# Loading the second half of batch 0's k through GpSimd's queue with a cast, instead of through ScalarE's queue and a ScalarE cast

## The chip, the core and the metric

The kernel runs on one core of a Trainium2 chip. The core has TensorE (PE in the profile, with its weight loads as PEld), VectorE (DVE), ScalarE (ACT), GpSimd (POOL) and SyncE (SP), and 16 DMA engines that serve the queues of all of them. The metric is the time of one execution in device microseconds; lower is better. The shown runs of the kernel before have a median of 292.75 us (eleven runs, 292.6 to 294.3).

## The reference

An attention without softmax is followed by a layer-normalised two-layer network. All inputs and the output are float32.

```python
# q, k, v: (8 batches, 8 heads, 576 rows, 64)
kv  = einsum('bhsd,bhse->bhde', k, v)
out = einsum('bhsd,bhde->bhse', q, kv)
rms = sqrt(mean(out * out, axis=-1) + 1e-06)
attn = out / rms * g_norm
# x: attn with its heads joined, (8, 576, 512)
xn = (x - mean(x)) / sqrt(var(x) + 1e-06) * g_ln
out = x + maximum(xn @ w_ch1, 0.0) @ w_ch2        # 512 -> 2048 -> 512
```

For each head, `kv` needs every row of k and of v before q can be multiplied with it. So nothing of a batch but its transposes can start before its k and v are on the chip.

## The kernel before

TensorE works in bfloat16 and the inputs are float32, so each input is cast on its way. Nearly all of it is cast by the DMA itself: a load that GpSimd issues reads float32 from memory and writes bfloat16. Only batch 0's k is loaded otherwise. It goes as float32 into the tile `k_f`, by the hardware queues of SyncE (line 124, heads 0 to 3) and ScalarE (line 125, heads 4 to 7). VectorE casts the first half into `k_p` (line 467) and ScalarE the second (line 468). `k_p` and `v_p` are views of the bfloat16 tiles `k_in[0]` and `v_in[0]`. `pairs` (line 117) gives the access pattern of one half: 128 partitions with two runs of 2,304 bytes each, which are 256 packets and 576 KB of float32.

The order of every engine's instructions is the order of the program text (a manual schedule). At the start GpSimd issues, one after the other: the two halves of batch 0's v (lines 126 and 127), two parts of its q (line 129), the first quarter of the weights w1 (`load_w1(0)`, line 130), an identity matrix for transposes, the rest of q (line 132), and three more quarters of w1. Then come w2's first half, the loads of batch 1, and w2's second half (lines 157 to 161). A load waits for the landing of the load eight before it in the same kind of queue. SyncE issues, after `k_f`, two small rows: `gl_row` (line 141) and `gn_row` (line 145), the weights of the two norms. VectorE clears tiles meanwhile (lines 123 to 155). After its half of the cast it spreads the two rows over the partitions (lines 470 and 471).

TensorE begins with 18 matmuls on a cleared tile whose results nobody reads (`fill(18)`, line 475). Then `kv_first` (line 207) makes batch 0's kv in two halves: the first of heads 0 to 3, from the first halves of k and v, the second of heads 4 to 7. Each half is copied out by VectorE (lines 222, 224, 225) and ScalarE (line 223). Then q is transposed (`turn_groups`, line 177) and multiplied with kv (`half_o`, line 494), the sums of squares are made, and by 15.7 us the first matmul with w1 runs (line 402). From there to the end the two matmul loops of the network, `mm1` (line 392) and `mm2` (line 439), fill TensorE, and the attention of the later batches is planned into them by slots (`at`, `tick`).

The tile `k_f` takes a buffer of the pool `m1pool`, whose two buffers later hold the network's hidden layer.

Of the kernel before, what the change touches and what calls it, by code (L numbers as in the profile page):

```python
# [14 lines left out]
def kernel(  # L15
# [11 lines left out]
    nc = tc.nc  # L27
    f32 = mybir.dt.float32
# [5 lines left out]
    B, H, S, D = q.shape  # L34
# [5 lines left out]
    HP = H // 2  # L40
# [3 lines left out]
    J, JJ, JP = 4, 5, 9  # L44
# [9 lines left out]
    m1pool = ctx.enter_context(tc.tile_pool(name="m1pool", bufs=2))  # L54
# [23 lines left out]


    NP = HP * JP * D  # L80
    k_f = m1pool.tile([128, HP, JP * D], f32, tag="m1", name="k_f")
    k_p, v_p = (t.rearrange("p h j d -> p (h j d)")[:, :NP].rearrange(
        "p (hp n) -> p hp n", hp=HP) for t in (k_in[0], v_in[0]))
    gl_row = work.tile([128, Dm], f32, tag="sq", name="gl_row")
# [32 lines left out]
    def pairs(t, hp0, hp1):  # L117
        return bass.AP(tensor=t.tensor, offset=t.offset + hp0 * 2 * S * D,
                       ap=[[JP * D, 128], [2 * S * D, hp1 - hp0], [1, JP * D]])
# [1 line left out]
    fill_sb = consts.tile([128, 512], bf16)  # L121
    gate = consts.tile([1, 1], bf16)
    nc.vector.memset(fill_sb, 0.0)
    nc.sync.dma_start(k_f[:, :HP // 2], pairs(k, 0, HP // 2))
    nc.scalar.dma_start(k_f[:, HP // 2:], pairs(k, HP // 2, HP))
    nc.gpsimd.dma_start(v_p[:, :HP // 2], pairs(v, 0, HP // 2))
    nc.gpsimd.dma_start(v_p[:, HP // 2:], pairs(v, HP // 2, HP))
    for h0 in (0, H // 2):
# [335 lines left out]
        clock[0] += 1  # L464


    nc.vector.tensor_copy(k_p[:, :HP // 2], k_f[:, :HP // 2])
    nc.scalar.copy(k_p[:, HP // 2:], k_f[:, HP // 2:])
    del k_f
    nc.vector.stream_shuffle(g_norm_sb[:, 0, :], gn_row, [0] * 32)  # L470
    nc.vector.stream_shuffle(g_ln_sb, gl_row, [0] * 32)
# [212 lines left out]
```

## Time and profile before

| what | value |
|---|---|
| median of the shown runs | 292.75 us |
| time of the profiled execution | 292.96 us |
| its span, first to last instruction | 291.2 us |
| mean granted TensorE clock | 0.998 |
| TensorE matmul busy | 283.8 us, 97% of the span |
| ScalarE busy | 154.8 us, 53% |
| VectorE busy | 151.0 us, 52% |
| GpSimd busy | 41.2 us, 14% |
| moved by DMA | 35.84 MB, mean 123 GB/s |
| of it by GpSimd's queue | 17.76 MB |
| of it by SyncE's queue | 16.99 MB |
| of it by ScalarE's queue | 0.72 MB |

The span is 1.8 us shorter than the profiled execution's time; what lies outside it is the launch and the end of the program. In the profile, q0 is the queue of GpSimd (software), q1 that of SyncE and q10 that of ScalarE (hardware). The bytes of a DMA are counted on the side that it writes, so a casting load of 590 KB of float32 counts 288 KB. "Idle before" in an instruction's row is time that its engine stood still before it, with the work that ended last among what it waited for.

### The profile page before, as it was taken

Reading aid. Unit: us, or ns where it says so; the run is one execution under the profiler, and the core shown is the slowest. Engines: PE = TensorE matmul, PEld = TensorE weight load, DVE = VectorE, ACT = ScalarE, POOL = GpSimd, SP = SyncE. Lnnn points to the kernel's source line nnn. Section 1 sums busy time; section 2 is a strip of 40 time slices with the busy share of each in tenths; the row PEclk is TensorE's granted clock in tenths of the full one; section 3 lists DMA queues with packets and bytes.
Section 4 is the critical chain, followed back from the end, with each engine's and each line's share of the span. In section 5 each row is a group of like instructions: output and inputs, shape, how many; then the busy total and the mean of one; then the engine's idle time right before and its main releaser. Section 6 shows DMA issues by size and latency. Waiting matters only on the chain.

```text
span 291.2 us, 5801 instructions
## 1 busy us (share of the span) xinstructions
PE 283.8 (97%) x2320; PEld 159.1 (55%) x2320; DVE 151.0 (52%) x335; ACT 154.8 (53%) x341; POOL 41.2 (14%) x68
## 2 busy tenths in 40 slices
PE   8889999999999999999999999999999999999995
PEld 3579755995578644444444444444444444444444
DVE  5775028826996793765276936661678200220022
ACT  3467754985569832882188418920894066016500
POOL 8523520041050003100320023000000000000000
PEclk9999999999999999999999999999999999999999
DMA  7999999469799619993998279959202510131033
GB/s 216 203 206 202 200 202 221 98 110 192 144 146 202 98 37 158 211 166 70 155 202 127 56 146 201 147 78 164 54 18 56 108 36 0 38 80 28 0 74 72
DMA packets 63290, 35.84 MB, mean 123 GB/s; under 512 B 30748, under 2 KB 58268, under 8 KB 63264
## 3 DMA queue, kind: packets, MB, share of 16 engines
q0 software_dynamic: 28016, 17.76, 44.9%
q1 hardware_dynamic: 34736, 16.99, 29.3%
q10 hardware_dynamic: 512, 0.72, 0.7%
q8 instruction: 18, 0.29, 0.4%
q14 instruction: 8, 0.07, 0.1%
HBM read 36.71 MB, written 9.44 MB: 158 GB/s over the span
## 4 chain that ended last, share of the span: by engine, by line
PE 80%; DMA 7%; DVE 6%; ACT 2%; issue 2%; SPq 1%; POOL 0%; DVEq 0%; POOLq 0%
PE p L402 40%; PE p L418 33%; DMA qt<-q_p 4%; PE o_ps L260 2%; DMA v_in<-in_v_dram 2%; PE kv_ps L235 2%; DVE o_sb L423 1%; DVE ss L287 1%; DVE x_blk L311 1%; DVE y L292 1%; DMA out_dram<-o_sb 1%; ACT m L405 1%; PE tp L183 1%; DVE xc L321 1%; PE p L196 1%
## 5 line engine op out<-in xcount | busy, mean ns | idle before, releaser
L402 PE MATMUL p<-xT_blk,w_sb 128*128 128x128 bf16 (+2 forms) x1024 | 132.0, 286 | 0.5 <-ACT m L405 0.3
L418 PE MATMUL p<-w_sb,m 128*128 128x512 bf16 (+2 forms) x608 | 130.2, 368 | 0.0
L405 ACT ACTIVATE m<-p 128x512 bf16<-128x512 f32 x144 | 85.3, 597 | 45.2 <-PE p L402 43.4
L402 PEld LDWEIGHTS <-w_sb 128*128 128x128 bf16 x1024 | 78.6, 98 | 45.5 <-issue 1.1
L418 PEld LDWEIGHTS <-m 128*128 128x128 bf16 x608 | 56.5, 98 | 60.3
L423 DVE SCALAR_TENSOR_TENSOR o_sb<-p,rstd,x_blk 128x512 f32<-128x512 f32 (+2 forms) x38 | 27.3, 719 | 44.2 <-PE p L418 41.5
L266 ACT ACTIVATE sq<-o_ps 128x512 f32<-128x512 f32 x34 | 20.2, 594 | 39.0 <-PE o_ps L260 39.0
L287 DVE TENSOR_REDUCE ss<-sq 128x8 f32<-128x512 f32 x34 | 23.2, 682 | 19.9 <-ACT sq L266 19.9
L329 ACT ACTIVATE dev<-x_blk,st_blk 128x512 f32<-128x512 f32 x36 | 25.8, 718 | 6.2 <-DVE st_blk L315 6.1
L321 DVE SCALAR_TENSOR_TENSOR xc<-x_blk,st_blk,g_ln_sb 128x512 bf16<-128x512 f32 x34 | 25.6, 752 | 1.2
L292 DVE TENSOR_TENSOR y<-o_ps,inv 128x512 f32<-128x512 f32 x34 | 23.5, 692 | 2.6
L311 DVE SCALAR_TENSOR_TENSOR x_blk<-y,g_norm_sb 128x512 f32<-128x512 f32 x34 | 23.5, 692 | 1.2
L411 DVE RECIPROCAL rstd<-rstd 128x4 f32<-128x4 f32 x9 | 1.6, 175 | 39.3 <-ACT rstd L410 39.3
L304 DVE RECIPROCAL inv<-rms 128x8 f32<-128x8 f32 x36 | 7.2, 200 | 22.5 <-ACT rms L297 22.4
L98 POOL COPY gate<-qt 1x1 bf16<-1x1 bf16 x5 | 0.9, 178 | 115.1 <-DMA qt<-q_p 115.1
L297 ACT ACTIVATE rms<-ss,eps_sb 128x8 f32<-128x8 f32 x36 | 10.8, 300 | 7.8 <-DVE ss L287 7.1
L260 PEld LDWEIGHTS <-qt 128*128 128x128 bf16 (+1 forms) x152 | 9.7, 100 | 8.5 <-DMA qt<-q_p 2.1
L260 PE MATMUL o_ps<-kv_pack,qt 128*128 128x128 bf16 (+1 forms) x152 | 13.3, 221 | 0.6 <-DMA qt<-q_p 0.3
L196 PE MATMUL p<-fill_sb 128*128 128x512 bf16 x28 | 9.2, 491 | 1.2 <-DVE eps_sb L137 1.2
L339 ACT COPY xT_blk<-tp 128x512 bf16<-128x512 bf16 x10 | 5.8, 579 | 2.3 <-PE tp L337 2.3
L329 ACT ACTIVATION_READ_ACCUMULATOR dev<-x_blk,st_blk 128x1 f32 x36 | 6.9, 193 | 0.0
L238 ACT CAST kv_pack<-kv_ps 64x256 bf16<-64x256 f32 x7 | 2.6, 366 | 7.9 <-PE kv_ps L235 7.8
(79 smaller groups left out, 119.0 us busy)
## 6 DMA issues: line engine op xcount, KB each, us to landing
out_dram<-o_sb SPq DMA_DIRECT2D x70, 128.0 KB, 2.5
w_sb<-in_moe_w_ch_dram POOLq DMA_DIRECT2D x8, 512.0 KB, 14.1
k_in<-in_k_dram POOLq DMA_DIRECT2D x7, 320.0 KB, 5.2
v_in<-in_v_dram POOLq DMA_DIRECT2D x7, 320.0 KB, 9.0
q_in<-in_q_dram POOLq DMA_DIRECT2D x7, 320.0 KB, 13.2
q_in<-in_q_dram POOLq DMA_DIRECT2D x8, 256.0 KB, 12.6
k_in<-in_k_dram POOLq DMA_DIRECT2D x7, 256.0 KB, 6.7
v_in<-in_v_dram POOLq DMA_DIRECT2D x7, 256.0 KB, 11.9
```

The costliest lines, as they stand in the source:

```text
L196: nc.tensor.matmul(p1, lhsT=fill_sb[:, :128], rhs=fill_sb, start=True, stop=True)
L260: nc.tensor.matmul(flat[rows, hp * 128:(hp + 1) * 128], lhsT=lhsT_of(hp), rhs=kvp[:, hp, :], start=True, stop=True)
L266: nc.scalar.activation(self.sq_t, self.o_ps, func=AF.Square)
L287: nc.vector.tensor_reduce(self.ss, self.sq_t, axis=AX.X, op=ALU.add)
L292: nc.vector.tensor_mul(self.y_t, self.o_ps, self.inv().to_broadcast([128, H, D]))
L311: nc.vector.scalar_tensor_tensor(x_blk[:, ts].rearrange("p (h d) -> p h d", h=H), in0=self.y_t, scalar=1.0, in1=g_norm_sb.to_broadcast([12 ...
L321: nc.vector.scalar_tensor_tensor(self.xc_t, in0=x_blk[:, self.ts], scalar=st[:, 1, self.ts:self.ts + 1], in1=g_ln_sb, op0=ALU.add, op1=ALU ...
L329: nc.scalar.activation(dev, x_blk[:, ts], func=AF.Square, bias=st[:, 1, ts:ts + 1], accum_out=st[:, 2, ts:ts + 1])
L402: nc.tensor.matmul(p1[:, i, :], lhsT=w1_sb[:, kk, de * 128:(de + 1) * 128], rhs=blk[2][:, kk, sl], start=(kk == 0), stop=(kk == nK - 1))
L405: nc.scalar.activation(m1[:, de0:de0 + per, sl], p1, func=AF.Relu)
L418: nc.tensor.matmul(p2[:, c0:c1], lhsT=m1s[b][:, de, ts * 128:(ts + 1) * 128], rhs=w2_sb[:, de, c0:c1], start=(de == 0), stop=(de == nDe - 1))
L423: nc.vector.scalar_tensor_tensor(o_sb[:, c0:c1], in0=p2[:, c0:c1], scalar=rstds[b][:, ts:ts + 1], in1=blks[b][0][:, ts, c0:c1], op0=ALU.mu ...
```

## The change

The second half of batch 0's k is loaded by GpSimd's queue, straight into the bfloat16 view, ahead of v. ScalarE neither issues that load nor casts. `k_f` holds only the first half.

```diff
-    k_f = m1pool.tile([128, HP, JP * D], f32, tag="m1", name="k_f")
+    k_f = m1pool.tile([128, HP // 2, JP * D], f32, tag="m1", name="k_f")
...
-    nc.sync.dma_start(k_f[:, :HP // 2], pairs(k, 0, HP // 2))
-    nc.scalar.dma_start(k_f[:, HP // 2:], pairs(k, HP // 2, HP))
+    nc.sync.dma_start(k_f, pairs(k, 0, HP // 2))
+    nc.gpsimd.dma_start(k_p[:, HP // 2:], pairs(k, HP // 2, HP))
     nc.gpsimd.dma_start(v_p[:, :HP // 2], pairs(v, 0, HP // 2))
     nc.gpsimd.dma_start(v_p[:, HP // 2:], pairs(v, HP // 2, HP))
...
-    nc.vector.tensor_copy(k_p[:, :HP // 2], k_f[:, :HP // 2])
-    nc.scalar.copy(k_p[:, HP // 2:], k_f[:, HP // 2:])
+    nc.vector.tensor_copy(k_p[:, :HP // 2], k_f)
     del k_f
```

In the changed program TensorE's second half of `kv_first` waits for that GpSimd load where it waited for ScalarE's cast. Every later load of GpSimd's queue is one place further back in it, and still waits for the load eight before it, which is the same load as before for all from w1's last quarter on. The orders of TensorE's, VectorE's and SyncE's instructions are unchanged, and so is ScalarE's but for the two that fall away.

## The prediction

> **What bounds the kernel now.** I read the shares of busy time first. TensorE is busy 283.8 of 291.2 us, so 7.4 us of the span are its idle time. What the change touches ends before 10 us, so I went to the chain that ended last, in order of time (start, length, what):
>
> ```profile
> 1.25 0.82 POOL v_in L126
> 2.07 6.84 DMA v_in<-in_v_dram
> 8.91 0.04 issue
> 8.95 0.19 PE even L219
> 9.71 0.44 PE tp L183 x16
> ```
>
> The chain runs through the second half of v, issued by GpSimd at 2.07 and landed at 8.91. ScalarE and k are not on it. The timeline of the start says why (start, length, engine and line; in brackets the idle time before, and who ended it):
>
> ```profile
> 0.76 0.49 ACTq L125 DMA_DIRECT2D k_f<-in_k_dram  x1
> 1.21 6.71 PE L196 MATMUL p<-fill_sb 128*128 128x512 bf16 x18 [1.21 <-DVE eps_sb L137]
> 5.62 1.00 DVE L467 CAST k_in<-k_f 128x1152 bf16<-128x1152 f32 x1 [1.20 <-DMA k_f<-in_k_dram]
> 5.98 1.15 ACT L468 CAST k_in<-k_f 128x1152 bf16<-128x1152 f32 x1 [3.20 <-DMA k_f<-in_k_dram]
> 8.63 0.28 DVE L222 CAST kv_pack<-even 64x128 bf16<-64x128 f32 x1 [0.30 <-PE odd L219]
> 8.95 0.19 PE L219 MATMUL even<-v_in,k_in 64*64 64x64 bf16 x1 [0.36 <-DMA v_in<-in_v_dram]
> ```
>
> The first half of kv starts at 7.84, when the filling matmuls end. By then its k is cast (5.62 + 1.00 = 6.62), and its v has landed (issued 1.25, 6.2 us to landing: 7.45). It ends at about 8.58. The second half stands still until v lands. ScalarE's cast was done at 7.13, that is 1.8 us before it was needed. **Its removal is worth nothing by itself.** What counts is how fast the four transfers k0, k1, v0, v1 (the halves of k and v, 256 packets each) go through the 16 DMA engines.
>
> So I read the DMA queues in short stretches. These are 4 to 5 us, then 5.1 to 5.3, then 5.3 to 5.5 (packets, MB, share of 16 engines):
>
> ```profile
> q10 hardware_dynamic: 92, 0.21, 53.5%
> q1 hardware_dynamic: 90, 0.20, 50.5%
> ...
> q10 hardware_dynamic: 37, 0.09, 107.5%
> q1 hardware_dynamic: 6, 0.00, 1.7%
> ...
> q0 software_dynamic: 20, 0.02, 66.5%
> q10 hardware_dynamic: 26, 0.03, 41.5%
> ```
>
> Up to 5.3 us the engines carry only the two halves of k. GpSimd's v, issued at 1.25, has not one packet before; then it takes over with no gap, and from 5.5 us runs at 35 to 36 packets in 0.2 us, 180 per us. The engines are full from 3.1 us, and the second v is simply the last of 1,024 packets.
>
> **The change part by part.**
>
> *Removed: ScalarE's load issue (0.49 us) and cast (1.15 us).* Nothing of ScalarE is waited for before line 223 at 8.66, which waits for TensorE. Worth 0.
>
> *Moved: k1 to the head of GpSimd's queue.* GpSimd's issues take 0.83, 0.74, 0.65, 0.65 and 0.80 us, so v, q and w1 are issued about 0.75 us later: v1 at 2.82 instead of 2.07, the first q at 3.55 instead of 2.79, the identity ready by about 6.2 instead of 5.4 (needed at 9.71). Is a later issue a later landing? Not while a queue of packets stands ahead. v1's turn comes after 6 us, 3 us after its new issue, and a software load that finds idle engines starts quickly: issued at 62.72, no packet until 64.0, 17 packets by 64.3, full rate by about 65.2. That is 1.3 us to the first packet and 2.5 us to full rate. Cost 0 while the queue is never empty; 0.75 us at most if it were.
>
> *The transfers.* The bytes read are the same: 4 x 590 KB. The order is now k0 | k1, v0, v1. k0 has the engines to itself at first. From the stretches of 0.2 us, its queue sent 6, 10, 9, 26 and 22 packets from 1.7 to 2.7, 73 in all. The other 183 at 180 per us take 1.02 us: k0 is through at 3.72. k1, issued at 1.25, should have first packets ready at 2.6 and full rate at 3.75, so it takes over there. The 768 packets of k1, v0, v1 at 180 per us take 4.27 us, to 7.99. By the same counting v0 and v1 ended before at 5.35 + 512/180 = 8.19, and landing came at 8.91, 0.72 later. So v1 lands at 7.99 + 0.72 = 8.71, **0.20 us earlier**. The gain is a dip that may go: when ScalarE's queue joined, the engines were half empty (2.75 to 3.00 us; the columns are length, busy times of PE, PEld, DVE, ACT, POOL, clock, DMA share, GB/s).
>
> ```profile
> 2.75:3.00 0.25, 0.25 (x2) 0.11 (x1) 0.25 (x2) 0.03 (x1) 0.25 (x2) 1.00 0.54 157
> 3.50:3.75 0.25, 0.25 (x3) 0.01 (x1) 0.15 (x2) 0.00 (x0) 0.25 (x1) 1.00 1.05 415
> ```
>
> Bounds: if one hardware queue alone never exceeds its best stretch (26 in 0.2 us, 130 per us), k0 ends at 4.1 and v1 lands at 9.1, +0.2. On the other side TensorE can't start its second half before 8.58, so no more than -0.37 is gained. I take -0.20, near the middle, since the full rate was reached each time two queues had packets.
>
> *What follows.* The first q landed at 2.79 + 6.9 = 9.7, just when TensorE turned to it (9.71). It is next in the same stream and moves along, as do w1 and the rest. w1's first quarter lands at 4.03 + 9.0 = 13.0 and is needed at 15.4. k0 lands near 4.3, and VectorE's cast starts when its clears end (4.42), not at 5.62; the path doesn't feel it, the filling matmuls cover it. The wait that takes the place of ScalarE's cast is for k1's landing, about 3.72 + 256/180 + 0.72 = 5.9; TensorE needs it at 8.6 or later. Behind that wait stands all of TensorE, so if k1 were late, everything would be.
>
> *The two small rows of SyncE.* The row of g_norm was issued at 2.46 and its spreading on VectorE started at 7.42: it too stood behind v. With k1 and v0 around it, I expect it at 5.5 to 7.5. If it fell behind v1 as well (about 8.4), VectorE's two spreads (0.23 and 0.73 us) would end at 9.4 instead of 8.3, and line 222 would start 0.8 late; the slack before line 225 and the copies at 11.10 takes most of it. Cost at most 0.3, taken as 0.
>
> **Rules weighed against the trace.** *DMA: Bandwidth & Descriptors* (the Trainium skill, section Queues, rings and completion order) says each engine takes turns between the queues that have work, a packet at a time. The rows above show no turn for q0 in 2.7 us, though a software load needs 1.3 us to its first packet; they look like service in order of arrival. By the rule, k0 and k1 share from 2.6 us and both end near 5.2; by the rows k0 ends at 3.7. v1 is last of 1,024 packets either way: by the rule -0.1 to 0, by the rows -0.20. I take the rows.
>
> *SBUF — State Buffer* (section SBUF: two separate sides) speaks against putting more on GpSimd: a float32 copy of VectorE within SBUF can lock GpSimd out, so that it cannot write DMA descriptors. The cast of line 467 is one, 1.00 us long. Beside it in this trace, at 6.05, three w1 issues took 2.47 us, 0.82 each, against 0.80 for the first w1 issue before it: no stop is seen. By the rule, issues at 4.4 to 5.4 (second q, w1) slip by up to 1.0 us; they have 2 us and more of packets ahead, so the sum is the same. If such a lock fell on k1 itself, it would be the next case.
>
> **The sum.** 0 - 0.20 + 0 = -0.20 us: span 291.0, time 292.76 against the profiled 292.96, which is 0.21 above the median. On the median: 292.55. It carries to the end one to one, since after 9 us the chain is 80% TensorE.
>
> **The rivals.**
>
> *A, slower: GpSimd's stream isn't ready when k0 is through.* Before, k1's 256 packets on ScalarE's queue covered the start of the software queue; that cover is gone. For: the trace shows no q0 packet before 5.3, so nothing proves it ready sooner at the program's very start. Against: it took over at full rate with no ramp, so it had been waiting. If its first packet can't come before 5.3, v1 lands at 5.35 + 4.27 + 0.72 = 10.34, and TensorE starts 1.4 us later: 294.15. It decides from a start at 3.95 on (8.95 - 0.72 - 4.27); +0.6 is reached at 4.55.
>
> *B, the full gain.* The engines lose nothing, and the filling matmuls become the bound: -0.37, 292.4. For: the dip above. Against: a single queue's slow first 0.6 us.
>
> *C, shifts later on.* 7.4 us of TensorE idle time and 11 us of the chain in transfers of qt (3.9%) hang on how loads and transposes meet after 100 us; a shift of 0.2 us there may turn into 0.6 to 1 either way, 292.0 or 293.5. No row shows such an echo.
>
> **Chances.** The forecast with its bounds (-0.3 to +0.2) 0.48, A 0.25, B 0.12, C 0.15 (half each way). A change within 0.2%, 0.59 us, is about what a measurement of this kernel can tell from none. A falls mostly outside it, C mostly. Faster 0.10, same 0.62, slower 0.28. The range runs from C's better end, 292.1, to 293.8, which takes in most of A.
>
> **What would show it.** In the new profile: no ScalarE cast; q0's first packets at 3.6 to 4.0 us at full rate; VectorE's cast near 4.4; v1 landed near 8.7, and the second half of kv right behind. A gap in the DMA share around 4 us, or v1 landing after 9.5, is A. A line 222 held by VectorE's spreads would say the small rows came late.

## The result, and the profile after

| | before | after |
|---|---|---|
| median of the runs | 292.93 us (47 runs, 292.59 to 294.58) | 296.3 us (12 runs, 295.27 to 297.81) |
| profiled execution, its span | 292.96, 291.2 us | 295.98, 294.2 us |
| mean granted TensorE clock | 0.998 | 0.994 |
| second half of kv starts on TensorE | 8.95 us | 11.29 us |
| first matmul with w1 (line 402) | 15.69 us | 18.91 us |

The changed kernel is slower: the ratio is 1.0112, with a 95% interval of 1.0098 to 1.0126. The forecast was 292.55, and its range ended at 293.8.

The chain that ended last, in order of time, now reads (start, length, what):

```profile
1.25 0.83 POOL k_in L125
2.08 0.71 POOL v_in L126
2.79 8.45 DMA v_in<-in_v_dram
11.24 0.04 issue
11.29 0.19 PE even L219
...
12.08 0.51 PE tp L183 x16
```

It is the same chain with one load more ahead of v1. That load shifts v1's issue by 0.72 us, from 2.07 to 2.79, and its time from issue to landing grows by 1.61 us, from 6.84 to 8.45. The timeline (start, length, engine and line, in brackets the idle time before and who ended it) shows what TensorE does meanwhile:

```profile
4.34 0.75 DVE L467 CAST k_in<-k_f 128x1152 bf16<-128x1152 f32 x1
6.55 0.81 PE L196 MATMUL p<-fill_sb 128*128 128x512 bf16 x3
9.39 0.19 PE L219 MATMUL even<-v_in,k_in 64*64 64x64 bf16 x1 [2.02 <-DMA v_in<-in_v_dram]
11.29 0.19 PE L219 MATMUL even<-v_in,k_in 64*64 64x64 bf16 x1 [1.15 <-DMA v_in<-in_v_dram]
```

TensorE runs out of filling matmuls at 7.36 and stands still twice, 2.02 us for v0 and 1.15 us for v1. ScalarE's cast is gone and VectorE's runs at 4.34, and both are without effect. So the question is why the loads are late, and the DMA queues answer it. First three stretches of 0.2 us, from 3.7, 4.1 and 6.1 us (packets, MB, share of 16 engines; a packet counts with its whole time where it starts, so a share can exceed 100%):

```profile
q0 software_dynamic: 19, 0.02, 66.6%
...
q0 software_dynamic: 25, 0.03, 183.4%
...
q0 software_dynamic: 32, 0.04, 122.6%
```

GpSimd's stream takes over from SyncE's as early as forecast. But it doesn't run at 35 packets in 0.2 us. It sends 19 and 25 in the first two of these stretches, and at 4.1 us they take longer: 183.4% of 16 engines for 0.2 us is 5.87 us for 25 packets, 235 ns each, against 123 ns at 6.1. In the packet records, which list every packet's start and length, most packets of the stream still take 107 ns, as before the change. The difference comes from **a few very long ones**: 31 took over 250 ns in the stream's first 5 us, 6 of them over 600 ns, the longest 1,331 ns. Before the change there is none over 107 ns in that time. (A few long packets alone are not special to GpSimd: at the start of k's hardware packets, from 1.86 us, 13 took over 250 ns before the change, the longest 521.) The records don't name a packet's engine, but they show that the 16 engines drift apart. Behind each load stand 16 packets of 4 bytes, which I read as one completion for each engine's share. Before, those of v0 came within 0.32 us, from 6.74 to 7.06. Now the first 16, which belong to k1 if the engines stay in order, run from 5.16 to 6.86, and k1 landed at 7.92. A load has landed when its slowest engine has.

The other loss is in the granted clock. Stretches of 0.5 us (length, busy times of PE, PEld, DVE, ACT, POOL, granted clock, DMA share, GB/s):

```profile
12.00:12.50 0.50, 0.46 (x19) 0.38 (x16) 0.41 (x2) 0.32 (x2) 0.45 (x2) 0.80 1.27 211
12.50:13.00 0.50, 0.50 (x6) 0.21 (x3) 0.45 (x2) 0.50 (x2) 0.50 (x1) 0.50 1.20 201
...
15.00:15.50 0.50, 0.50 (x8) 0.50 (x6) 0.23 (x2) 0.50 (x3) 0.20 (x1) 0.50 1.45 240
15.50:16.00 0.50, 0.50 (x7) 0.38 (x6) 0.50 (x2) 0.29 (x2) 0.48 (x1) 0.78 1.15 188
```

After its two pauses TensorE runs at half clock (0.50 in the column before the last two) from about 12.3 to 15.7 us, just where the transposes and `half_o` lie. Before, the clock was 1.00 in these stretches. From the second half of kv to the first w1 matmul it takes 7.62 us instead of 6.74, 0.88 more. So 2.34 us for v1's landing plus 0.88 make the 3.22 us by which line 402 starts late; 0.2 of it is won back until the end of the span.

### The profile page after: what moved, and what is told of

Its sections match the earlier page's. It is cut to its first block, busy times and chain, and to the rows that moved or that the text cites. A ratio compares the mean times of both kernels' runs of the same rounds, so it can differ in the third digit from the quotient of the medians.

```text
span 294.2 us, 5798 instructions
## 1 busy us (share of the span) xinstructions
PE 284.6 (97%) x2320; PEld 160.0 (54%) x2320; DVE 150.7 (51%) x335; ACT 153.5 (52%) x340; POOL 41.7 (14%) x69
## 4 chain that ended last, share of the span: by engine, by line
PE 82%; DVE 6%; DMA 6%; ACT 3%; issue 2%; POOL 1%; SPq 0%; DVEq 0%; POOLq 0%
PE p L402 40%; PE p L418 36%; DMA v_in<-in_v_dram 3%; PE o_ps L260 2%; DMA qt<-q_p 2%; PE kv_ps L235 2%; DVE o_sb L423 1%; DVE ss L287 1%; DVE x_blk L311 1%; DVE y L292 1%; DMA out_dram<-o_sb 1%; ACT m L405 1%; PE tp L183 1%; DVE xc L321 1%; ACT sq L266 0%
```

## The experiments

Fifteen kernels were run. None leaves out any work; where one does extra work (a load that nobody reads, clears, filling matmuls), it is said. The table gives what the packet records show of GpSimd's stream: its first packet, the time from this to the start of its 256th, the packets over 250 and over 600 ns in its first 5 us. Then come the start of kv's second half on TensorE, the median and the ratio to the kernel before with its interval. All but the last two columns come from one profiled execution of each kernel. In e3, e4, e5, e6, e7, e8, e9 and e11 it was the fastest on record, in e10 the slowest, so it need not show what made the median.

| kernel | hardware packets of k (or cover) ahead | first packet, us | 256 packets in, us | over 250 / 600 ns | kv, second half, us | median, us | ratio [95%] |
|---|---|---|---|---|---|---|---|
| before | 512 | 5.33 | 1.51 | 0 / 0 | 8.95 | 292.93 | 1 |
| e6, VectorE casts all | 512 | 5.29 | 1.58 | 0 / 0 | 8.95 | 292.96 | 1.0002 [0.9994, 1.0011] |
| e1, all k by SyncE | 512 | 4.98 | 1.77 | 6 / 0 | 9.57 | 293.25 | 1.0016 [1.0002, 1.0029] |
| e7, v issued 0.8 later | 512 | 5.29 | 1.67 | 4 / 0 | 9.26 | 294.06 | 1.0041 [1.0026, 1.0056] |
| e8, v issued 2.1 later | 512 | 5.26 | 1.61 | 14 / 1 | 9.37 | 294.6 | 1.0077 [1.0048, 1.0106] |
| e2, changed + cover | 512 | 5.12 | 1.87 | 1 / 0 | 10.41 | 295.67 | 1.0082 [1.005, 1.0115] |
| e10, changed + half the cover | 384 | 4.40 | 1.94 | 27 / 3 | 11.02 | 295.84 | 1.0092 [1.0063, 1.0121] |
| after, the changed kernel | 256 | 3.56 | 2.57 | 31 / 6 | 11.29 | 296.3 | 1.0112 [1.0098, 1.0126] |
| e12, queue moved, no DMA cast | 256 | 3.81 | 3.27 | 29 / 8 | 10.67 | 295.37 | 1.0078 [1.005, 1.0106] |
| e14, v0 ahead of k1 | 256 | 3.71 | 2.33 | 28 / 4 | 10.96 | 295.53 | 1.0106 [1.008, 1.0133] |
| e3, VectorE idle | 256 | 3.74 | 2.63 | 29 / 8 | 10.76 | 296.17 | 1.0105 [1.0055, 1.0155] |
| e9, GpSimd writes nothing | 256 | 3.53 | 2.49 | 17 / 7 | 10.91 | 295.78 | 1.0095 [1.0071, 1.012] |
| e4, TensorE kept busy | 256 | 3.65 | 2.65 | 31 / 6 | 11.69 | 295.84 | 1.0105 [1.0077, 1.0133] |
| e13, all loads about 1 us later | 256 | 4.54 | 1.77 | 21 / 0 | 11.29 | 295.13 | 1.008 [1.006, 1.01] |
| e15, all loads over 4 us later | 256 | 7.99 | 1.81 | 27 / 7 | 14.62 | 297.94 | 1.0147 [1.0068, 1.0226] |
| e11, k1 late, engines idle before | 256, then a pause | 5.99 | 2.19 | 20 / 1 | 12.22 | 297.89 | 1.0166 [1.0139, 1.0194] |
| e5, all k by GpSimd | 0 | 2.79 | 1.85 | 35 / 6 | 11.24 | 297.26 | 1.0157 [1.014, 1.0174] |

### The parts of the change alone

**e6, only the cast is taken from ScalarE** (against the kernel before):

```diff
-    nc.scalar.copy(k_p[:, HP // 2:], k_f[:, HP // 2:])
+    nc.vector.tensor_copy(k_p[:, HP // 2:], k_f[:, HP // 2:])
```

> The kernel before with both casts of k on VectorE; loads unchanged. It removes ScalarE's cast alone. All theories but one: no change, 292.6 to 293.3, v1 lands at 8.9. Rival A2 (a cast of VectorE holds up GpSimd's descriptors, and two casts twice as long): GpSimd's issues beside the casts take 1 us and more, v1 or the first q lands over 0.5 us later, time 293.5 or more.

The time is that of the kernel before. The casts ran at 5.69 and 6.54 us on VectorE and ended at 7.48, before TensorE was ready for them. What the change set out to remove was worth nothing, as its price of 0 in the prediction had it.

**e12, only the queue** (against the kernel before; k1 stays float32, and ScalarE casts it):

```diff
-    nc.scalar.dma_start(k_f[:, HP // 2:], pairs(k, HP // 2, HP))
+    nc.gpsimd.dma_start(k_f[:, HP // 2:], pairs(k, HP // 2, HP))
```

> The kernel before, with one word changed: the second half of k goes through GpSimd's queue instead of ScalarE's, but still as float32 into k_f, and ScalarE casts it as before. It is the move to the other queue without the cast in the DMA. If the software queue at that place is what is slow: stalled packets from 3.7 to 5.6 us, v1 lands at 10.7 to 11.6, time 295 to 297. If the cast in the transfer (2,304 bytes read, 1,152 written) is what is slow at the start: k1 at full rate, v1 lands at 9.0 to 9.5, time 292.8 to 293.6.

Eight packets over 600 ns, the longest 1,716, and 295.37 us. **The move to GpSimd's queue brings the long packets and most of the loss by itself; the cast in the transfer isn't needed for it.**

**e1, k1 leaves ScalarE's queue, but for SyncE's** (against the kernel before):

```diff
-    nc.scalar.dma_start(k_f[:, HP // 2:], pairs(k, HP // 2, HP))
+    nc.sync.dma_start(k_f[:, HP // 2:], pairs(k, HP // 2, HP))
```

> The kernel before, with both float32 halves of k on SyncE's queue; casts as before. Theory C (cover: GpSimd's stream starts slowly, and the 512 hardware packets of k in front of it hide that): two queues or one make no difference, 512 packets still stand in front, v1 lands at 8.7 to 9.2 us, time 292.6 to 293.3. Rival Q (what counts is that ScalarE's second queue feeds the engines at the start): v1 lands after 10 us, time 294 or more.

1.0016 [1.0002, 1.0029]: near the kernel before. One hardware queue carries 512 packets about as well as two (the last starts at 5.41 us, before at 5.50), and v follows with six packets over 250 ns, the longest 414. In the profiled execution, one of the slower of twenty (294.48), v1 landed at 9.53, past the expected 9.2, yet before the rival's 10. So it isn't ScalarE's queue that is missed, but hardware packets ahead of the stream.

**e5, the opposite end: all of k by GpSimd** (against the changed kernel; VectorE casts nothing either):

```diff
-    nc.sync.dma_start(k_f, pairs(k, 0, HP // 2))
+    nc.gpsimd.dma_start(k_p[:, :HP // 2], pairs(k, 0, HP // 2))
     nc.gpsimd.dma_start(k_p[:, HP // 2:], pairs(k, HP // 2, HP))
```

> The changed kernel with k's first half loaded by GpSimd's queue with a cast too: no hardware packet in front of the software stream, no cast on any engine. Theories C: the slow start begins at 2.6 us, with the first load; the first 2 us at 100 packets per us, the rest of 1,024 at about 155: last packet at 9.9, v1 lands at 10.6, not later than in the changed kernel (11.2). Rival D (every 256 packets moved from the hardware to the software queue cost their 2.3 us): v1 lands at 13.5, time 298.5 or more.

kv's second half starts at 11.24, no later than in the changed kernel, though its first packet isn't a hardware one (v1 landed at 11.20, against 10.6 expected; the first q, one place further back, landed at 12.12). But one thing fits no expectation: k0, the first load on idle engines, went through quickly (256 packets in 1.85 us), and the slow stretch came with the loads behind it, 4.9 to 7.3 us. So the slow part isn't always at the very start of the stream.

### Does a cover bring the stream back?

**e2, a useless hardware load in the place of the old one.** 576 KB of batch 1's k go to ScalarE's queue into a half of `k_f` that nobody reads (against the changed kernel, with `k_f` at its full size again):

```diff
+    nc.scalar.dma_start(k_f[:, HP // 2:], pairs(k, H // 2, H // 2 + HP // 2))
     nc.gpsimd.dma_start(k_p[:, HP // 2:], pairs(k, HP // 2, HP))
```

> The changed kernel, plus a hardware load of 576 KB on ScalarE's queue that nobody uses (from batch 1's k, into the unused half of k_f). Theory C: the 256 packets more keep the engines busy until 5.3 us, GpSimd's stream then runs at 180 packets per us, and v1 lands at 5.35 + 4.27 + 0.72 = 10.3 us, 0.9 EARLIER than in the changed kernel although 590 KB more are read before it; time about 295 (or less, with less of the clock lost). Rival V (VectorE locks GpSimd out of writing descriptors until 5.1 us): the descriptors are late all the same; also near full rate from 5.3, so not told apart here. Rival S (a k or v load through GpSimd is slow by itself, 155 packets per us, wherever it stands): v1 lands at 5.35 + 768/155 + 0.72 = 11.0 or, with the measured start, 12 us or more; time 296.5 to 297.5.

The load adds 256 packets ahead of everything, and yet **v1 is there sooner: kv's second half starts at 10.41 instead of 11.29**. The stretches of 0.5 us from 5.5 and 6.0 of this kernel:

```profile
q0 software_dynamic: 73, 0.08, 97.5%
q10 hardware_dynamic: 20, 0.02, 12.8%
...
q0 software_dynamic: 92, 0.11, 123.0%
```

92 packets in 0.5 us are the 180 per us of the kernel before, right from the takeover, and one packet is over 250 ns. The completions of each load come within 0.5 us again. That the total falls only to 295.67 is mostly the clock's doing: in the profiled execution it is 0.50 from 11.07 to 17.9 us, and from kv's second half to the first w1 matmul it takes 8.52 us instead of 6.74. (The first q, behind 256 more packets, landed at 11.20, when kv's second half was just through.) The one execution of e2 at clock 1.0 took 294.35, 0.9 below that of the changed kernel at that clock.

**e10, half of that cover** (128 packets; against e2):

```diff
-    nc.scalar.dma_start(k_f[:, HP // 2:], pairs(k, H // 2, H // 2 + HP // 2))
+    nc.scalar.dma_start(k_f[:, HP // 2:HP // 2 + 1], pairs(k, H // 2, H // 2 + 1))
```

> The changed kernel with a useless hardware load of 128 packets (288 KB of batch 1's k) on ScalarE's queue, half of that of the covering run. GpSimd's turn comes at about 4.4 us instead of 3.7 (changed) or 5.4 (covering run). Theory C1 (lead of k1 about 3.2 us): q0 a little slow at its start, 70 to 85 packets per 0.5 us, v1 lands near 10, and the time is the lowest of the three, 294.5 to 295.5. If the cover works by its size and not by the lead, the packets stay as slow as in the changed kernel to 6 us and v1 lands at 11 or later, 296 to 297.

In the profiled execution it misses v1 near 10: 27 packets over 250 ns and 11.02 us. There half of the cover helps little. But this was the slowest of four, 296.32; the one at clock 1.0 took 294.27, no more than e2's, and its packets aren't on record. So whether half a cover fails each time is open.

### What makes the start slow?

**e3, VectorE kept idle** from 1.8 to 7.6 us (against the changed kernel): its clears are moved behind the loads, and ScalarE does its cast.

```diff
-    nc.vector.tensor_copy(k_p[:, :HP // 2], k_f)
+    nc.scalar.copy(k_p[:, :HP // 2], k_f)
```

> The changed kernel with VectorE idle from 1.8 us to the spreading of the small rows: ScalarE casts k's first half, the clears come after the spreads (those for later batches at slot 7.5). Rival V: GpSimd's stream runs at 180 packets per us from 3.7 us on, v1 lands at 8.7 to 9.2, time 292.8 to 293.5. Theory C: the slow start is as it was (about 100 packets per us from 3.7 to 5.6), v1 lands at 10.8 to 11.4, time 295.5 to 296.8. In between: each has its part.

VectorE does nothing from 1.77 to 7.50 us, and the stream is as slow and has as many long packets. So it isn't VectorE's work.

**e9, GpSimd kept from writing descriptors** (a clear of a part of w2's tile from 3.5 to 6.2 us, against the changed kernel):

```diff
     nc.gpsimd.dma_start(v_p[:, HP // 2:], pairs(v, HP // 2, HP))
+    nc.gpsimd.memset(w2_sb[:, :6, :], 0.0)
```

> The changed kernel, with a GpSimd clear of a part of w2's tile right after the issue of v's second half, so that GpSimd writes no descriptors between about 3.5 and 6.3 us; q and w1 are issued some 2.8 us later. Theory P (the writing of descriptors for the loads behind it disturbs the packets of k1 and v): q0 runs at 160 per us or more from 4.5 us on, v1 lands at 9.5 or before, and then q is what comes late. Theory C1 (lead time only): packets as in the changed kernel, about 100 per us to 5.6 us, v1 lands at 10.8 to 11.5, time 296 to 297.5, as q comes later too.

Seven packets over 600 ns fall in that very stretch. So it isn't the writing of the descriptors of the loads behind. The time is the changed kernel's, though q and w1 were issued 2.3 to 2.8 us later.

**e7 and e8, v issued later in the kernel before.** A clear ahead of v's issue (`:3` in e7, `:6` in e8) leaves v less lead before its turn at 5.3 us:

```diff
+    nc.gpsimd.memset(w2_sb[:, :6, :], 0.0)
     nc.gpsimd.dma_start(v_p[:, :HP // 2], pairs(v, 0, HP // 2))
```

> The kernel before, with a clear of 1,536 elements per partition on GpSimd ahead of its first load (it clears part of w2's tile, which is loaded later), so that v is issued some 1.5 us later, at about 2.8 and 3.6 us; all 512 hardware packets of k still stand in front and are through at 5.35. Theory C1 (what the cover gives is time: a software load needs some 4 us from its issue until all 16 engines have its packets ready): the time from issue to takeover falls from 4.1 to 2.5 us, nearly the 2.3 us of the changed kernel; the stream starts slowly, v1 lands at 10 to 11 us, time 294 to 295.5. Rival C2 (what the cover gives is that the engines or the memory have been warmed by hardware traffic, whenever the software load was issued): the stream takes over at 5.35 at full rate, v1 lands at 8.9 to 9.2, time 292.8 to 293.2.

> The kernel before, with a GpSimd clear of a part of w2's tile (twice that of the late-issue run) ahead of its first load, so that v is issued at about 3.5 and 4.2 us, with all of k by hardware as before. Theory C1 (a software load runs at full rate only if it was issued some 4 us before its turn; here the lead is about 1.9 us, less than k1's 2.4 in the changed kernel): q0's packets come slow and uneven after 5.3 us, v1 lands at 10 or later, time 294.3 to 296. Theory C2 (the chip's DMA is slow for software packets in the first 6 to 7 us of a program, whenever they were issued, and well later): the packets come from about 5.3 to 6 on and are at full rate from 6.5, v1 lands at 9.0 to 9.5, 292.9 to 293.7.

In e8 v0 is issued at 3.35 us, 1.9 us before its turn; k1 in the changed kernel is issued 2.3 us before its own. Still v0's packets come at full rate: 90 and 88 in the half microseconds from 5.5 and 6.0.

```profile
q0 software_dynamic: 90, 0.10, 120.4%
q10 hardware_dynamic: 3, 0.00, 1.4%
...
q0 software_dynamic: 88, 0.10, 123.7%
```

**So a short lead alone doesn't make the stream slow**; kv's second half starts at 9.37, inside the second expectation. It may not be without effect: 14 packets over 250 ns follow, 11 of them behind v0, where the kernel before has none. And the profiled execution, 293.57, is the fastest of four. The median, 294.6, lies in the first expectation (294.3 to 296), and no kept trace shows what the slower ones lost. e7 is divided likewise: 9.26 us, near its second expectation, but a median of 294.06, just in the range of its first.

**e14, other data in the slow place** (against the changed kernel):

```diff
-    nc.gpsimd.dma_start(k_p[:, HP // 2:], pairs(k, HP // 2, HP))
     nc.gpsimd.dma_start(v_p[:, :HP // 2], pairs(v, 0, HP // 2))
+    nc.gpsimd.dma_start(k_p[:, HP // 2:], pairs(k, HP // 2, HP))
```

> The changed kernel with v's first half ahead of k's second half in GpSimd's queue (v0, k1, v1). Theory K (k's second half is slow to read by this queue, wherever it stands): v0's 256 packets go in 1.5 to 1.9 us, and the stalls over 600 ns come after 5.3 us, with k1. If it is the place and not the data: 2.4 to 2.7 us for v0's 256 packets, stalls over 600 ns from 3.7 us on as in the changed kernel, v1 lands at 10.8 to 11.6 and the time is 295 to 297. The first half of kv has its v somewhat earlier, and doesn't set the end.

v0 is now as slow as k1 was. It is the place, not the data.

**e11, e13 and e15, the time since the program's start.** In e11 a clear of GpSimd delays its loads alone, so the engines fall idle after k0. In e13 and e15 one or four clears of `k_f` stand ahead of SyncE's k0 as well, so that the loads keep their order (and 8 or 18 more filling matmuls run). Of e15:

```diff
+    for _ in range(4):
+        nc.gpsimd.memset(k_f, 0.0)
     nc.sync.dma_start(k_f, pairs(k, 0, HP // 2))
```

> The changed kernel with a GpSimd clear of a part of w2's tile ahead of k1's load, so that k1, v0 and v1 are issued at about 4.1, 4.9 and 5.6 us, 2.9 us later than in the changed kernel, and the engines stand idle after k0 is through at 3.7. Theory T (software packets stall only in the first 5 us or so of the program): first packets near 5.4, full rate from about 6.5, few packets over 250 ns; v1 lands between 10.4 and 11.5, no later than in the changed kernel although it is issued 2.9 us after. Theory M (the stream stalls whenever fewer than 512 hardware packets ran before it, at whatever time): stalls of about 1 us again, 100 packets per us for two microseconds, and v1 lands at 12.5 to 14, time 297.5 or more. Either way the time is above the changed kernel's or equal to it, since q comes later too.

> The changed kernel moved later as a whole: a GpSimd clear of the float32 tile stands ahead of k0's load and of all GpSimd loads, so that k0 is issued near 2.5 us and k1 near 2.6 instead of 0.75 and 1.25 (8 more filling matmuls keep TensorE busy). The order and the distance of the loads stay as in the changed kernel. Theory T (software packets stall in the first 5 us or so of the program): k1's turn comes near 5.6, its 256 packets go in 1.5 to 1.9 us as v0's did before, no stall over 600 ns. Theory M (a software stream that has fewer than 512 hardware packets ahead of it is slow, at whatever time): 2.4 to 2.7 us for the first 256 packets and several stalls over 600 ns, as in the changed kernel. The time is no evidence, since everything starts about 2 us later: 296 to 300.

> As the shifted run, but with four such clears ahead of k0 and of GpSimd's loads (and 18 more filling matmuls than in the changed kernel), so that k0 and k1 are issued at about 5 us and k1's turn comes near 7.7. Order, distance and lead of the loads stay. Theory T (it is the time since the program's start): k1's 256 packets go in 1.5 to 1.7 us, no packet over 600 ns and at most a few over 250 ns, and the other 512 in 2.9 us. Theory M or a short lead (it is what ran before, or how long before its turn a load was issued): 2.3 to 2.7 us for the first 256 packets and several packets over 600 ns, as at 3.6 us in the changed kernel; the 1.77 us of the run shifted by 1 us was then chance. The time is no evidence: everything starts some 4 us later, 297 to 302.

e13 alone spoke for "only the first microseconds of a program": no packet over 600 ns. But its clear took 1.06 us, and GpSimd's loads were issued only 0.5 us later. e15, moved by about 4 us, refutes it. Its stretch of 0.5 us from 9.5:

```profile
q0 software_dynamic: 67, 0.06, 144.3%
q1 hardware_dynamic: 8, 0.01, 5.2%
```

67 packets instead of 90, with 172 ns each (144.3% of 8 us of engine time). Seven of the stream's packets, from 9.59 to 10.02 us, took over 600 ns, the longest 1,309. The long packets move along with the stream. In e15 those seven come 1.6 to 2.0 us after its first packet, in the changed kernel the six come 0.6 to 1.2 us after it. e11 lies between its two expectations: 12.22 instead of at most 11.5, one packet over 600 ns.

**The same start later in the kernel before.** If it belongs to the start of GpSimd's stream, the profile of the kernel before must have it too, wherever this queue starts after a pause. Its packet records do:

| first packet after a pause, us | packets in the 2 us from there | over 250 / 600 ns | longest | over 250 / 600 ns in the next 2 us |
|---|---|---|---|---|
| 5.33 (behind 512 hardware packets) | 358 | 0 / 0 | 107 ns | 0 / 0 |
| 64.12 | 385 | 16 / 3 | 913 ns | 2 / 0 |
| 84.48 | 400 | 12 / 3 | 721 ns | 0 / 0 |
| 115.15 | 227 | 24 / 8 | 1,021 ns | 1 / 0 |
| 144.57 | 347 | 13 / 5 | 871 ns | 7 / 1 |
| 174.40 | 258 | 20 / 9 | 978 ns | 3 / 2 |

Five of the six starts have the long packets. The one at 5.33 hasn't. (The later packets are of 640 bytes and usually take 69 ns, those at 5.33 of 1,152 bytes and 107 ns.) So the best reading is that the changed kernel doesn't disturb a healthy stream: it loses the one start that cost nothing, and gets the ordinary one, where TensorE waits for it.

The table also shows what does not suffice as a cover. In the 5 us up to the start at 115.15, SyncE's queue kept the engines busy (transposes and stores of the output):

```profile
q1 hardware_dynamic: 2623, 0.88, 90.4%
```

Still 24 long packets followed. So neither a count of hardware packets nor busy engines hide the start by themselves.

### The clock

**e4, filling matmuls in TensorE's pauses** (against the changed kernel; 8 more ahead of kv, and 5 between its halves):

```diff
         for i in range(HP // 2):
+            if i:
+                fill(5)
...
-    fill(18)
+    fill(26)
```

> The changed kernel with 8 more filling matmuls ahead of kv and 5 between its two halves, so that TensorE doesn't stand idle; loads as in the changed kernel. If the clock of 0.5 from 12.3 to 15.6 us comes from TensorE's standing idle and cost 0.9 us: v1 still lands near 11.2, the clock stays 1.0, the first w1 matmul comes at 18.0 instead of 18.9, time 295.4. If the clock is not the idleness's doing or costs nothing: 296.3 as in the changed kernel.

The first of the two expectations holds in its mechanism. One pause is left, ahead of kv's first half, and the clock stays 1.00:

```profile
9.82 0.19 PE L221 MATMUL even<-v_in,k_in 64*64 64x64 bf16 x1 [1.52 <-DMA v_in<-in_v_dram]
...
12.50:13.00 0.50, 0.42 (x17) 0.38 (x18) 0.49 (x2) 0.32 (x2) 0.24 (x2) 1.00 1.30 198
```

From kv's second half to the first w1 matmul it takes 6.87 us (11.69 to 18.56), near the 6.74 of the kernel before. **So it was the pauses that took the clock**, but not any pauses. The profiled execution of e9 stood still twice as well, and kept it:

```profile
9.17 0.19 PE L220 MATMUL even<-v_in,k_in 64*64 64x64 bf16 x1 [1.30 <-DMA v_in<-in_v_dram]
10.91 0.19 PE L220 MATMUL even<-v_in,k_in 64*64 64x64 bf16 x1 [0.99 <-DMA v_in<-in_v_dram]
...
12.50:13.00 0.50, 0.50 (x18) 0.39 (x18) 0.11 (x1) 0.40 (x2) 0.50 (x2) 1.00 1.20 188
```

It took 6.71 us for the same work. In e1, 1.43 and 0.73 us were enough to lose the clock; which pauses cost it is open. In e4 v1 landed at 11.54, 0.3 later than in the changed kernel, and the filling matmuls held kv's second half up a little more, which is part of why the median falls only to 295.84. The fastest run of the changed kernel, at clock 1.0, took 295.27, 2.3 above the kernel before. That agrees with the profile: of its 3.4 us some 2.3 are the late loads, and the rest is clock.

No version here beats the kernel before. Its second half of kv starts at 8.95 and can't start before 8.58, where the first half ends, so that at most 0.37 us was to be had at this place.

## Why the prediction was wrong

*ScalarE's cast and issue, 0: right.* e6 shows it alone: 1.0002 [0.9994, 1.0011].

*k0 through at 3.72, and k1 taking over there: right.* GpSimd's first packet comes at 3.56, when SyncE's 256 are nearly through, and none before. So the reading "in order of arrival" fits better than the rule of turns as the prediction took it.

*The full rate from there on: wrong, and this is the failed step.* The prediction put it as "it takes over there. The 768 packets of k1, v0, v1 at 180 per us take 4.27 us, to 7.99". Measured, the 384th of them starts at 6.98 instead of 5.85, and the last at 10.38 instead of 7.99. About 1.1 us is rate: the first 256 took 2.57 us, 100 per us. The 31 long packets took 11.7 us more than the usual 107 ns each, 0.73 us for each of the 16 engines. Some 1.3 us more is spread: the engines are out of step, and a load is done with the last. 302 packets of q had started before the last one of v1; before the change it was 37. Then 0.86 us to the landing (0.72 was forecast): 11.24 instead of 8.71.

*Why I got it wrong.* I had the right row, the load issued at 62.72 with its full rate only at 65.2, but read it as a delay after the issue, which 2.5 us in the queue would have used up. e15, and the profiled execution of e8, speak against this. In e8 1.9 us of lead behind 512 hardware packets was enough for v0. In e15 2.9 us behind 256 was not. And I took the smooth takeover at 5.3 as the stream's nature ("it took over at full rate with no ramp, so it had been waiting"). It was the exception among six starts in that same trace. To look at the other five would have shown it.

*GpSimd's later issues, 0: right as far as tried.* The loads behind v1 were covered by the same queue of packets; in e9 they came over 2 us later still, and the time did not rise.

*The cast against GpSimd's writing.* The first two q issues, beside VectorE's cast, took 1.74 us instead of 1.29; with ScalarE casting (e3) they took 1.29. In e14 the same issues took 1.29 beside the cast, and the cast 0.97 us instead of 0.75; in e9 the cast, beside GpSimd's clear, took 2.48. So something like the lock that the prediction weighed is there, where it had seen no stop, and either of the two can be held up. It isn't what made the loads late: e3 has the same late loads without it.

*The small rows: right.* VectorE's spread began at 7.10 (5.5 to 7.5 was forecast) and nobody waited for it. *VectorE's cast:* 4.34 (4.42).

*The rivals.* A was the nearest: GpSimd's stream not ready when k0 is through, without k1's cover. Its direction and place were right. Its form was not: I had thought of a late first packet followed by full rate (v1 at 10.34, 294.15), and what came was an early first packet and a slow, uneven stream. B and C didn't appear; the loss is whole by line 402 and doesn't grow later.

*Not foreseen at all: the clock.* The prediction counted TensorE's pauses once, as waiting. They cost again, 0.88 us, in the half clock behind them. That two pauses of such lengths lose the clock was not certain beforehand, as e9 shows.

**What stays open.** Shown is that v1 lands late because GpSimd's stream is slow there, that the move to its queue does this without the cast (e12), that it doesn't hang on VectorE (e3), on the writing of further descriptors (e9), on the data (e14) or on the time since the program's start (e15), and that a hardware load which nobody needs takes it away (e2). That it is the ordinary start of this stream is the best reading of the six starts; e5, whose first load was quick and whose second and third were slow, and e13, with no packet over 600 ns, do not fit it well. Why 512 hardware packets ahead hide it and 256 don't is not shown. In these runs the time that the engines had been running goes with their number (3.1 to 3.5 us against 2.6 and less without a pause), and the start at 115.15 shows that traffic of another kind doesn't do the same. *DMA: Bandwidth & Descriptors* (the Trainium skill, section Terms) says that GpSimd writes its descriptors to rings in SBUF, while the hardware queues' descriptors are fed to the engines directly. Engines that get their descriptors late might leave such packets; no run here shows it.

## What to carry to other kernels

When a load is moved from a hardware queue to GpSimd's, ask what ran on the engines while GpSimd's stream started: here k1's hardware packets hid that start, and without them v was 2.3 us late, although the same bytes were read. Read every start of that queue in the trace, not only the one that the change touches. And weigh a pause of TensorE twice, as the wait itself and as a clock that may be lost after it (0.9 us here, 1.8 in e2); and first ask whether the work that is to go (here a cast with 1.8 us to spare) is waited for at all.

## What the runs showed of the hardware

- A start of GpSimd's stream after a pause: in its first 2 us 12 to 24 packets of over 250 ns, up to 1,021, where 107 and less is usual (five of six starts of the kernel before).
- A useless hardware load of 256 packets ahead (e2) made the software loads behind it land sooner (10.41 instead of 11.29 us).
- With the 16 engines in step, their completions of one load lay within 0.32 us; out of step, the first 16 lay 1.7 us apart, and k1, v0 and v1 took 6.7 to 8.5 us from issue to landing.
- Two pauses of TensorE of 2.02 and 1.15 us, with 0.75 us of matmuls between them, were followed by some 3.4 us at half clock. *TensorE: Matmul & The Clock Gate* (the Trainium skill, section HAM oscillation) gives the rule as no idle gaps over about 3.4 us. Here no single gap was that long. In e14 gaps of 0.36 and 2.67 us lost the clock, and in e1 1.43 and 0.73; 1.52 in e4, and 1.30 and 0.99 in e9, did not.
